# Reading turned expert outputs back over 128 rows, one scaling and scatter per step, in a fused attention and expert kernel

## The chip, the core and the metric

One core of a Trainium2 chip runs the whole program. The metric is device microseconds of one execution. Names used below: PE is the matrix engine and PEld its weight load, DVE the vector engine, ACT the scalar engine, POOL the GpSimd engine, SP the engine that issues most transfers (DMAs).

## The reference, cut to what matters

A gated linear attention feeds a gated feed-forward block, and that feeds a mixture of 8 experts. The change touches the last stage alone:

```python
def _moe2_ref(x, w_gate, w_output_gate, w1, w2):      # x: 3072 tokens x 384, 8 experts, F = 1024
    ...
    e_idx = np.argmax(logits, axis=1)                 # each token goes to one expert
    for e in range(E):
        mask = e_idx == e
        h = np.maximum(x[mask] @ w1[e], 0.0)
        ye = h @ w2[e]
        out[mask] = gate_w[mask, None] * eom[mask, e, None] * ye
```

## The kernel before, in words

Attention, feed-forward and routing fill the first 600 us and are the same in both kernels. Routing writes every token's row, its gate and its token number into a table `bucket` in DRAM, sorted by expert.

**Parts.** The experts are then worked one after the other, the fullest first. `SLOTS` gives each a shape of rows x tiles: (128,4), (114,4), (108,4), (100,4), (118,3), (112,3), (128,3), (128,3). The first is worked in two halves, so there are nine parts u = 0 to 8, and part u is slot u - 1 from u = 1 on. Each part has 8 steps j. In a step PE makes a block of h (`e_h`: 9 matmuls, L650), ACT and DVE make its two halves with relu (L1166, L1167), and two steps later `e_o` multiplies that block by w2 into three or four PSUM banks `ps_b`. All products are made three times, from a high and a low half of each operand.

**Turned parts.** Where the rows are fewer than 128 (`TURNED`: parts 2 to 6) the output is made with the model dimension on the partitions (L1187), three banks of r*n columns. The banks' unused columns up to a multiple of 32 are set to zero (L1182). `turn_out` turns the banks in 32x32 blocks on DVE (L1209) and writes them with 8 transfers into a DRAM tile `mid_o` (L1212), at step 0 of the next part. `fetch_out` at step 3 of the next part reads them back, one tile `obr` of r partitions per transfer (L1222). `fin_out` at step 6 scales all n tiles by the gates (even ones on ACT, L1231; odd ones on DVE, L1233) and scatters each by its token numbers `ix` (L1235, an indirect DMA that POOL issues). The scalings are held in source order on their engines.

**Rows of the next part.** `load_rows` reads the next part's rows from `bucket` (4 transfers of 32 partitions, L1119, and one for gates and token numbers, L1122), at step 0 of the part before it. `prep_rows` at steps 3, 5 and 6 turns them on DVE (L1134) and splits them into high and low (`x`: ACT L1147, DVE L1148), for each of three blocks kc; with the last kc it casts the token numbers to integers (L1129).

**Weights.** Eight chunks of 384 KB per expert go through six staging buffers. A chunk of w1 is split on ACT and DVE (L1075, L1076), one of w2 on ACT and POOL (L1092, L1095); the splits of one step free the buffer for a later load.

**What sets the order.** A scheduler orders each engine's instructions by a simulated timeline; what is given to `keep_in_program_order` keeps its place in the source. Each engine works its list strictly in order, so an instruction that waits holds up all behind it on that engine.

Of the kernel before, what the change touches and what calls it, by code (L numbers as in the profile page):

```python
# [8 lines left out]
F32 = mybir.dt.float32  # L9
# [46 lines left out]
def gla_glu_moe_kernel(  # L56
# [996 lines left out]
    TURNED = [p for p, (r, n) in enumerate(SLOTS) if 0 < p < E - 1 and r < P]  # L1053
    we = {}
    ring = []
    turns = [0]

    def staging(nm, shape):
# [7 lines left out]
    def load_w1(p, i):  # L1066
        n = F2 // 4
        s = slice(i * n, i * n + n)
        st = staging("st1", [P, KD, n])
        nc.sync.dma_start(st, w1.rearrange("e k n -> (e k) n")[bass.ds(places[p][1], DM), s]  # L1070
                          .rearrange("(p kc) n -> p kc n" if p else "(kc p) n -> p kc n", p=P))

        def go():
            w1h, w1l = we[p][0:2]
            for ins in (nc.scalar.activation(w1h[:, :, s], st, AF.Copy),  # L1075
                        nc.vector.tensor_tensor(out=w1l[:, :, s], in0=st, in1=f(w1h[:, :, s]), op=ALU.subtract)):  # L1076
                if p:
                    tc.keep_in_program_order(ins)
        return go

    def load_w2(p, i):
        st = staging("st2", [P, 2, DM])
        nc.sync.dma_start(st, w2.rearrange("e k n -> (e k) n")[bass.ds(places[p][2], F2), :]
                          [i * 2 * P:(i + 1) * 2 * P, :].rearrange("(kc p) n -> p kc n", p=P))

        def go():
            w2h, w2l = (w_[:, 2 * i:2 * i + 2, :] for w_ in we[p][2:4])
            src = st
            if p in TURNED:
                w2h, w2l = (w_.rearrange("p a (k m) -> p a k m", k=KD) for w_ in (w2h, w2l))  # L1090
                src = st.rearrange("p a (m k) -> p a k m", k=KD)
            ins = nc.scalar.activation(w2h, src, AF.Copy)  # L1092
            if p:
                tc.keep_in_program_order(ins)
            nc.gpsimd.tensor_tensor(out=w2l, in0=src, in1=f(w2h), op=ALU.subtract)  # L1095
        return go
# [11 lines left out]
    def load_rows(u, er):  # L1108
        p, s0, r, n = parts[u]
        rows_ = bucket[bass.ds(places[p][0], CMAX), :]  # L1110
        ix = act.tile([P, 4, 1], I32, tag="ix", name="ix", bufs=4)
        if u < 2:
            nc.sync.dma_start(er[:, 0:n, :], rows_[s0:s0 + P * n, :].rearrange("(p b) w -> p b w", b=n))
            erow[u] = (er, ix, er[:, :, DM:DM + 1], er[:, :, RW - 1:RW])
            return
        m = -(-r * n // 32)
        flat_ = flat(er)[:, 0:3 * 32 * m]
        for i in range(TW):
            nc.sync.dma_start(flat_[32 * i:32 * i + 32].rearrange("j (c w) -> j c w", c=m),  # L1119
                              rows_[0:32 * m, 96 * i:96 * i + 96].rearrange("(c j) w -> j c w", j=32))  # L1120
        eg = act.tile([P, 4, 2], F32, tag="eg", name="eg", bufs=4)
        nc.sync.dma_start(eg[0:r, 0:n, :], rows_[0:r * n, DM:RW].rearrange("(b p) w -> p b w", b=n))  # L1122
        erow[u] = (flat_, ix, eg[:, :, 0:1], eg[:, :, 1:2])

    def prep_rows(u, kc):
        _, _, r, n = parts[u]
        er, ix, _, ids = erow[u]
        if kc == (0 if u < 2 else KD - 1):
            nc.vector.tensor_copy(ix[0:r, 0:n, :], ids[0:r, 0:n, :])  # L1129
        xh, xl = x2[u]  # L1130
        if u >= 2:
            m = er.shape[1] // 96
            tc.keep_in_program_order(
                nc.vector.transpose(out=xt[:, 0:32 * m].rearrange("p (c j) -> p c j", c=m),  # L1134
                                    in_=er.rearrange("p (c d k) -> p k c d", c=m, k=KD)[:, kc]))
            psf = xt[:, 0:r * n]
        else:
            if u == 1 and kc:
                ps = psM.tile([P, n, r], F32, tag=order[kc + 1], name="ps_t")
            else:  # L1140
                ps = psE.tile([P, n, r], F32, tag="tr", name="ps_t", bufs=1)
            for i in range(n):
                ins = nc.tensor.transpose(ps[:, i, :], er[0:r, i, kc * P:kc * P + P], ident[0:r, 0:r])
                if u == 0 and i == 0:
                    tc.keep_in_program_order(ins)
            psf = ps.rearrange("p b c -> p (b c)")
        for ins in (nc.scalar.activation(xh[:, kc, :], psf, AF.Copy),  # L1147
                    nc.vector.tensor_tensor(out=xl[:, kc, :], in0=psf, in1=f(xh[:, kc, :]), op=ALU.subtract)):  # L1148
            if u == 1:
                tc.keep_in_program_order(ins)  # L1150
# [20 lines left out]
    def e_o(u, j, tiles=None):  # L1171
        p, _, r, n = parts[u]
        turned = p in TURNED
        if u not in ob2:
            ob2[u] = []
            for i in range(KD if turned else n):
                ob2[u].append(psM.tile([P, -(-r * n // 32) * 32 if turned else DM], F32,
                                       tag=order[turn[0] % 5], name="ps_b"))
                turn[0] += 1
            if turned and r * n % 32:  # L1180
                for o in ob2[u]:
                    nc.vector.memset(o[:, r * n:], 0.0)  # L1182
        hh = h2[u, j]
        if turned:
            for k_ in range(KD):
                for m, (a_, b_) in enumerate(((0, 2), (0, 3), (1, 2))):
                    nc.tensor.matmul(ob2[u][k_][:, 0:r * n], lhsT=we[p][b_][:, j, k_ * P:k_ * P + P],  # L1187
                                     rhs=hh[:, a_, :], start=(j == 0 and m == 0), stop=(j == KF2 - 1 and m == 2))
            return
        for i in range(n) if tiles is None else tiles:  # L1190
            sl = slice(i * r, i * r + r)
            for m, (a_, b_) in enumerate(((0, 2), (0, 3), (1, 2))):
                ins = nc.tensor.matmul(ob2[u][i][0:r], lhsT=hh[:, a_, sl], rhs=we[p][b_][:, j, :],  # L1193
                                       start=(j == 0 and m == 0), stop=(j == KF2 - 1 and m == 2))
                if tiles is not None:
                    tc.keep_in_program_order(ins)
# [3 lines left out]

    def turn_out(u):
        p, _, r, n = parts[u]
        nb = -(-r * n // 32)
        mid = dram.tile([4 * P, DM], F32, tag="mid_o", name="mid_o", bufs=2)
        for c0 in range(0, nb, HB):
            nc_ = min(HB, nb - c0)
            ob = act.tile([P, HB, 96], F32, tag="R", name="obt")[:, 0:nc_, :]
            for k_ in range(KD):
                nc.vector.transpose(out=ob.rearrange("p c (d k) -> p k c d", k=KD)[:, k_],  # L1209
                                    in_=ob2[u][k_][:, 32 * c0:32 * (c0 + nc_)].rearrange("p (c j) -> p c j", c=nc_))  # L1210
            for a_ in range(TW):
                nc.sync.dma_start(mid[32 * c0:32 * (c0 + nc_), 96 * a_:96 * a_ + 96].rearrange("(c j) w -> j c w", j=32),  # L1212
                                  ob[32 * a_:32 * a_ + 32])
        ob2[u, "m"] = mid

    def fetch_out(u):
        p, _, r, n = parts[u]
        ob2[u, "s"] = []
        for i in range(n):
            ob = act.tile([P, DM], F32, tag=("t", "hh", "hl")[spare[0] % 3], name="obr")  # L1220
            spare[0] += 1
            nc.sync.dma_start(ob[0:r], ob2[u, "m"][i * r:i * r + r, :])  # L1222
            ob2[u, "s"].append(ob)

    def fin_out(u):
        p, _, r, n = parts[u]
        _, ix, gates, _ = erow[u]
        for i in range(n):
            ob = ob2[u, "s"][i][0:r]
            if i % 2 == 0:  # L1230
                ins = nc.scalar.activation(ob, ob, AF.Copy, scale=gates[0:r, i, :])  # L1231
# [212 lines left out]
    def load_next(p):  # L1444
        for i in range(4):
            pw.append((load_w1, p, i))
            pw.append((load_w2, p, i))
# [27 lines left out]
    for u in range(U):  # L1475
        for j in range(KF2):
# [21 lines left out]
                load_rows(2, ers[0])  # L1498
            if u == 0 and j == 3:
                strict[0] = False  # L1500
            if u > 1 and j == 0 and u + 1 < U:
                load_rows(u + 1, ers[(u + 1) % 2])
            if u > 1 and j == 3 and parts[u][0] + 2 < E:
                addresses(parts[u][0] + 2)
                load_next(parts[u][0] + 2)
            if u and parts[u - 1][0] in TURNED and j in (3, 6):
                (fetch_out if j == 3 else fin_out)(u - 1)
            if u and u + 1 < U and j in TRJ:
                prep_rows(u + 1, TRJ.index(j))
            for _ in range(STEPS[u][j] if u < 2 else 1):  # L1510
# [10 lines left out]
        if u == 1:  # L1521
            while ready or pw:
                weight_step()
            addresses(2)
            load_next(2)
            fetch()
    op_ = overflow()
# [42 lines left out]
```

## Time and profile before

| | us |
|---|---|
| median of 3 runs | 841.31 (840.16 to 842.48) |
| profiled execution | 842.69 |
| its span | 840.9 |
| PE busy in the span | 808.4 (96%) |
| DVE, ACT, POOL busy | 549.6, 326.2, 153.2 |

PE is the bound: nearly all of the span it is busy, so a change can gain only where PE stands still or runs at a lower clock. Since the profiled execution is 1.4 us above the median, a sum is made against 842.69 and then moved to the median. Row forms: in the timeline "start us, us, engine line operation tile<-source, xcount [idle before <-what ended it]"; merged rows give the start of the first and the time from there to the end of the last.

### The profile page before, as it was taken

How to read it: one execution, taken by the hardware profiler on the slowest of the kernel's cores; microseconds unless marked ns; L12 is line 12 of the kernel's file. 1: busy time of each engine (PE TensorE's matmuls, PEld its weight loads, DVE VectorE, ACT ScalarE, POOL GpSimd, SP SyncE). 2: the span in 40 equal slices, each digit the busy share in tenths (PEclk: the TensorE clock that was granted, in tenths of full speed). 3: DMA queues.
4: the chain of work that ended last, by engine and by line, in shares of the span. 5: the costliest groups of instructions: out<-in, count | busy, mean ns of one | idle time of the engine just before them, and what ended most of it. 6: DMA issues, size and time to landing. Idle time of an engine off the chain costs nothing.

```text
span 840.9 us, 15931 instructions
## 1 busy us (share of the span) xinstructions
PE 808.4 (96%) x5967; PEld 774.8 (92%) x5967; DVE 549.6 (65%) x1202; ACT 326.2 (39%) x694; POOL 153.2 (18%) x207
## 2 busy tenths in 40 slices
PE   6999999999999999999999999999999999984996
PEld 5799999998999999999999999999988999984896
DVE  7998999498677876767766742443554765672541
ACT  1655544323333333423333323333245454452341
POOL 3000000000200110010020020013124353452351
PEclk9999999999999999999999999999999999997899
DMA  9955564863554452235454210050078667674520
GB/s 196 203 157 147 155 149 129 227 173 78 143 118 102 119 124 70 70 93 117 89 134 89 54 48 20 1 187 11 29 218 222 165 189 210 190 217 136 165 70 27
DMA packets 193751, 106.00 MB, mean 126 GB/s; under 512 B 124489, under 2 KB 188421, under 8 KB 193673
## 3 DMA queue, kind: packets, MB, share of 16 engines
q1 hardware_dynamic: 189208, 95.50, 44.8%
q0 software_dynamic: 4464, 9.48, 3.3%
q8 instruction: 47, 0.77, 0.4%
q14 instruction: 32, 0.25, 0.1%
HBM read 80.37 MB, written 24.84 MB: 125 GB/s over the span
## 4 chain that ended last, share of the span: by engine, by line
PE 76%; issue 12%; POOL 5%; DMA 3%; DVE 1%; ACT 1%; SPq 1%; POOLq 0%; DVEq 0%; ACTq 0%
PE ps_o L684 18%; PE ps_g L650 18%; PE ps_v L650 18%; PE ps_h L650 5%; PE ps_s L430 4%; PE ps_b L1187 3%; PE ps_y L468 3%; PE ps_y L464 2%; POOL w2b L1095 2%; POOL out_dram L1235 2%; POOL w2a L1095 1%; PE ps_st L489 1%; PE ps_b L1193 1%; PE pc L615 1%; DMA nat<-in_k_dram 1%
## 5 line engine op out<-in xcount | busy, mean ns | idle before, releaser
L664 ACT ACTIVATE hh<-tt 128x384 fp32r<-128x384 f32 x96 | 50.5, 526 | 145.8 <-DVE tt L661 134.8
L661 DVE TENSOR_TENSOR tt<-tt,ps_v 128x384 f32<-128x384 f32 x96 | 52.9, 551 | 82.0 <-PE ps_v L650 69.9
L642 ACT ACTIVATE tt<-ps_g 128x384 f32<-128x384 f32 x96 | 47.0, 489 | 82.2 <-PE ps_g L650 76.5
L1167 DVE SCALAR_TENSOR_TENSOR h<-ps_h,h 128x256 fp32r<-128x256 f32 (+6 forms) x72 | 37.9, 529 | 49.7 <-ACT h L1166 46.9
L670 DVE TENSOR_TENSOR hl<-tt,hh 128x384 fp32r<-128x384 f32 x96 | 54.2, 564 | 24.6 <-ACT hh L664 23.6
L650 PE MATMUL ps_g<-xh,wgh 128*128 128x384 f32 x192 | 66.5, 347 | 0.0
L650 PE MATMUL ps_v<-xh,wvh 128*128 128x384 f32 x192 | 66.4, 346 | 0.0
L684 PE MATMUL ps_o<-wol,hh 128*128 128x400 f32 x192 | 66.3, 345 | 0.0
L650 PE MATMUL ps_g<-xl,wgh 128*128 128x384 f32 x192 | 64.7, 337 | 0.9 <-DVE begin L317 0.9
L684 PE MATMUL ps_o<-woh,hh 128*128 128x400 f32 x192 | 65.3, 349 | 0.0
L650 PE MATMUL ps_h<-x,w1a 128*128 128x256 f32 (+3 forms) x288 | 53.8, 331 | 11.8 <-ACT x L1147 11.5
L650 PE MATMUL ps_v<-xh,wvl 128*128 128x384 f32 x192 | 64.8, 338 | 0.0
L650 PE MATMUL ps_g<-xh,wgl 128*128 128x384 f32 x192 | 64.6, 337 | 0.0
L650 PE MATMUL ps_v<-xl,wvh 128*128 128x384 f32 x192 | 64.5, 336 | 0.0
L684 PE MATMUL ps_o<-woh,hl 128*128 128x400 f32 x192 | 64.0, 345 | 0.0
L1166 ACT ACTIVATE h<-ps_h 128x256 fp32r<-128x256 f32 (+6 forms) x72 | 33.7, 469 | 76.7 <-PE ps_h L650 75.0
L650 PEld LDWEIGHTS ps_h<-x,w1a 128*128 128x128 f32 x288 | 48.1, 192 | 13.7 <-ACT x L1147 11.8
L650 PE MATMUL ps_h<-x,w1b 128*128 128x456 f32 (+3 forms) x288 | 57.5, 342 | 0.0
L650 PEld LDWEIGHTS ps_h<-x,w1b 128*128 128x128 f32 x288 | 50.7, 188 | 1.5
L1187 PE MATMUL ps_b<-h,w2b 128*128 128x456 f32 (+2 forms) x216 | 45.2, 352 | 2.7 <-DVE ps_b L1182 2.7
L440 DVE TENSOR_TENSOR P<-ps_s,mask 128x512 f32<-128x512 f32 x46 | 30.1, 685 | 23.6 <-PE ps_s L430 23.6
L1187 PEld LDWEIGHTS ps_b<-h,w2b 128*128 128x128 f32 x216 | 39.6, 195 | 4.3 <-issue 2.9
(312 smaller groups left out, 2011.1 us busy)
## 6 DMA issues: line engine op xcount, KB each, us to landing
st<-in_moe_w_dram SPq DMA_DIRECT2D x46, 384.0 KB
bucket<-zero SPq DMA_DIRECT2D x8, 772.0 KB
stg<-in_moe_w_gate_dram SPq DMA_DIRECT2D x12, 384.0 KB
stg<-in_moe_w_val_dram SPq DMA_DIRECT2D x12, 384.0 KB
stg<-in_moe_w_out_dram SPq DMA_DIRECT2D x12, 384.0 KB
v<-in_v_dram SPq DMA_DIRECT2D x23, 192.0 KB
more<-in_moe_w_dram SPq DMA_DIRECT2D x9, 384.0 KB
er<-in_moe_w_dram SPq DMA_DIRECT2D x9, 384.0 KB
```

The costliest lines, as they stand in the source:

```text
L430: seq(nc.tensor.matmul(ps[hh][:, p, :], lhsT=kT[r, p, :], rhs=qT[r, p, :], start=True, stop=True))
L440: pace(f'Ph{t}', nc.vector.tensor_tensor(out=Ph, in0=ps[hh], in1=mb, op=ALU.mult))
L642: nc.scalar.activation(tt, ps, AF.Silu)
L650: seq(nc.tensor.matmul(ps, lhsT=a_[:, kc, :], rhs=b_[:, kc, :], start=(n == 0), stop=(n == 3 * KD - 1)))
L661: nc.vector.tensor_tensor(out=tt, in0=tt, in1=ps, op=ALU.mult)
L664: nc.scalar.activation(hh, tt, AF.Copy)
L670: nc.vector.tensor_tensor(out=hl, in0=tt, in1=f(hh), op=ALU.subtract)
L684: seq(nc.tensor.matmul(obank[s][i], lhsT=a_[:, sl], rhs=weight(b_, j), start=(j == j0 and n == 0), stop=(j == j1 - 1 and n == 2)))
L1095: nc.gpsimd.tensor_tensor(out=w2l, in0=src, in1=f(w2h), op=ALU.subtract)
L1166: nc.scalar.activation(hh[:, 0, :], ps, AF.Relu)
L1167: nc.vector.scalar_tensor_tensor(out=hh[:, 1, :], in0=ps, scalar=0.0, in1=f(hh[:, 0, :]), op0=ALU.max, op1=ALU.subtract)
L1187: nc.tensor.matmul(ob2[u][k_][:, 0:r * n], lhsT=we[p][b_][:, j, k_ * P:k_ * P + P], rhs=hh[:, a_, :], start=(j == 0 and m == 0), stop=(j = ...
```

## The change

1. `fetch_out` reads `mid_o` back in tiles of 128 partitions; partition p of tile i takes row p*n + i (before: row i*r + p, over r partitions). So that all 128*n rows exist, the banks are 128*n columns wide, zeroed from r*n on, and all of them are turned and written. The gates and token numbers of turned parts are read with the same layout.
2. `fin_out` scales and scatters one tile per step: at steps 4 to 7 where n is 4, at 5 to 7 where n is 3.
3. `load_rows` is called at step 7 for the part after the next (before: at step 0 for the next); part 3's stays at step 0 of part 2.
4. Transfers of weights (from slot 2 on), rows, `mid_o` and `obr` keep their source order on SP.
5. The cast of the token numbers is made at step 3 of their own part.
6. The address registers of slot 2 are loaded at step 3 of part 1.

```diff
@@ load_w1, load_w2
-        nc.sync.dma_start(st, w1...)
+        ins = nc.sync.dma_start(st, w1...)
+        if p > 1:
+            pin(ins)
@@ load_rows (its four reads of the rows are pinned too)
-        nc.sync.dma_start(eg[0:r, 0:n, :], rows_[0:r * n, DM:RW].rearrange("(b p) w -> p b w", b=n))
+        pin(nc.sync.dma_start(eg[:, 0:n, :], rows_[0:P * n, DM:RW].rearrange(
+            "(p b) w -> p b w" if p in TURNED else "(b p) w -> p b w", b=n)))
@@ prep_rows
-        if kc == (0 if u < 2 else KD - 1):
+        if u < 2 and kc == 0:
             nc.vector.tensor_copy(ix[0:r, 0:n, :], ids[0:r, 0:n, :])
@@ e_o
-                ob2[u].append(psM.tile([P, -(-r * n // 32) * 32 if turned else DM], F32,
+                ob2[u].append(psM.tile([P, P * n if turned else DM], F32,
-            if turned and r * n % 32:
+            if turned:
                 for o in ob2[u]:
                     nc.vector.memset(o[:, r * n:], 0.0)
@@ turn_out (its writes of mid are pinned too)
-        nb = -(-r * n // 32)
+        nb = TW * n
@@ fetch_out
-            nc.sync.dma_start(ob[0:r], ob2[u, "m"][i * r:i * r + r, :])
+            pin(nc.sync.dma_start(ob, ob2[u, "m"][0:P * n, :].rearrange("(p b) w -> p b w", b=n)[:, i, :]))
@@ fin_out
-    def fin_out(u):
+    def fin_out(u, i):
-        for i in range(n):
+        if 0 <= i < n:
@@ the loop over parts and steps
-            if u > 1 and j == 0 and u + 1 < U:
-                load_rows(u + 1, ers[(u + 1) % 2])
-            if u > 1 and j == 3 and parts[u][0] + 2 < E:
+            if u == 2 and j == 0:
+                load_rows(3, ers[1])
+            if u > 1 and j == 7 and u + 2 < U:
+                load_rows(u + 2, ers[u % 2])
+            if u > 1 and j == 3:
+                _, _, r, n = parts[u]
+                pin(nc.vector.tensor_copy(erow[u][1][0:r, 0:n, :], erow[u][3][0:r, 0:n, :]))
+            if u and j == 3 and parts[u][0] + 2 < E:
                 addresses(parts[u][0] + 2)
-                load_next(parts[u][0] + 2)
-            if u and parts[u - 1][0] in TURNED and j in (3, 6):
-                (fetch_out if j == 3 else fin_out)(u - 1)
+                if u > 1:
+                    load_next(parts[u][0] + 2)
+            if u and parts[u - 1][0] in TURNED and j > 2:
+                if j == 3:
+                    fetch_out(u - 1)
+                fin_out(u - 1, parts[u - 1][3] - KF2 + j)
```

On ACT in the second half of part 6 stands this before (h is the relu of a step, obr the scaling of a tile of part 5, x the high half of the rows of part 7, w1a and w2a splits of weights):

```order
L1166 ACTIVATE h_9057<-ps_h 128x336
L1166 ACTIVATE h_9086<-ps_h 128x336
L1231 ACTIVATE obr<-obr,eg 118x384 x2
L1147 ACTIVATE x_7160<-xt 128x384
L1092 ACTIVATE w2a<-st_8848 128x768
L1166 ACTIVATE h_9128<-ps_h 128x336
L1092 ACTIVATE w2a<-er_6553 128x768
L1147 ACTIVATE x_7160<-xt 128x384
```

and this in the changed kernel:

```order
L1175 ACTIVATE h_9057<-ps_h 128x336
L1240 ACTIVATE obr<-obr,eg 118x384
L1156 ACTIVATE x_7160<-xt 128x384
L1100 ACTIVATE w2a<-st_8854 128x768
L1175 ACTIVATE h_9090<-ps_h 128x336
L1156 ACTIVATE x_7160<-xt 128x384
L1081 ACTIVATE w1a_6547<-st_8906 128x3x256
L1175 ACTIVATE h_9123<-ps_h 128x336
L1240 ACTIVATE obr<-obr,eg 118x384
L1100 ACTIVATE w2a<-er_6553 128x768
```

The second scaling moved from ahead of two blocks of x to behind both.

On POOL, from the end of part 4 to the start of part 6, the list before is (DMA is a scatter, four of one part in a row):

```order
L1095 TENSOR_TENSOR w2b<-st_8549,w2b 128x768
L1235 DMA out_dram<-obr,ix 3072x384 x4
L1095 TENSOR_TENSOR w2b<-st_8624,w2b 128x768
L1095 TENSOR_TENSOR w2a<-er_6553,w2a 128x768
L1095 TENSOR_TENSOR w2a<-st_8777,w2a 128x768
```

and in the changed kernel:

```order
L1244 DMA out_dram<-obr,ix 3072x384 x2
L1103 TENSOR_TENSOR w2b<-st_8555,w2b 128x768
L1244 DMA out_dram<-obr,ix 3072x384
L1103 TENSOR_TENSOR w2b<-st_8623,w2b 128x768
L1244 DMA out_dram<-obr,ix 3072x384
L1103 TENSOR_TENSOR w2a<-er_6553,w2a 128x768
L1103 TENSOR_TENSOR w2a<-st_8785,w2a 128x768
```

The split of the fourth w2b chunk moved from behind the fourth scatter to ahead of it.

On DVE at the start of part 4 the list before is (obt is the turn of part 3's banks, ps_b a bank of part 4 or 5 that is zeroed):

```order
L1209 STREAM_TRANSPOSE obt<-ps_b 128x256
L1209 STREAM_TRANSPOSE obt<-ps_b 128x192
L1182 MEMSET ps_b 128x16
L1209 STREAM_TRANSPOSE obt<-ps_b 128x256
L1209 STREAM_TRANSPOSE obt<-ps_b 128x192
L1076 TENSOR_TENSOR w1a_6548<-st_8122,w1a_6547 128x3x256
L1182 MEMSET ps_b 128x30 x2
```

and in the changed kernel:

```order
L1218 STREAM_TRANSPOSE obt<-ps_b 128x256 x6
L1082 TENSOR_TENSOR w1a_6548<-st_8122,w1a_6547 128x3x256
L1191 MEMSET ps_b 128x112
L1191 MEMSET ps_b 128x30 x2
L1176 SCALAR_TENSOR_TENSOR h_8319<-ps_h,h_8319 128x400
```

The zeroing of part 4's third bank moved behind the split of a w1 chunk, where it already stood at the start of parts 5 and 6.

## Rows read from the trace of the kernel before

**Rows 1.** Timeline of PE, 670 to 841 us.
```profile
733.43 1.73 PE L650 MATMUL ps_h<-x,w1a 128*128 128x354 f32 x9 [0.28 <-DVE h L1167]
...
750.08 1.01 PE L1187 MATMUL ps_b<-h,w2b 128*128 128x336 f32 x5 [2.66 <-DVE ps_b L1182]
...
777.08 0.69 PE L650 MATMUL ps_h<-x,w1a 128*128 128x384 f32 x1 [11.47 <-ACT x L1147]
777.57 0.76 PE L1187 MATMUL ps_b<-h,w2b 128*128 128x336 f32 x2
778.12 0.84 PE L650 MATMUL ps_h<-x,w1a 128*128 128x384 f32 x2
778.76 2.72 PE L1187 MATMUL ps_b<-h,w2b 128*128 128x336 f32 x9
781.28 2.79 PE L650 MATMUL ps_h<-x,w1a 128*128 128x384 f32 x12
784.36 1.33 PE L1193 MATMUL ps_b<-w2a,h 128*128 128x384 f32 x6 [0.29 <-ACT h L1166]
...
788.84 1.73 PE L650 MATMUL ps_h<-x,w1a 128*128 128x384 f32 x9
790.41 1.74 PE L1193 MATMUL ps_b<-w2a,h 128*128 128x384 f32 x9
...
798.53 1.32 PE L1193 MATMUL ps_b<-w2a,h 128*128 128x384 f32 x6 [1.14 <-ACT h L1166]
```

**Rows 2.** Windows: length; PE, PEld, DVE, ACT, POOL busy (count); PE clock, DMA share, GB/s.
```profile
761.70:763.50 1.80, 1.80 (x13) 1.80 (x13) 0.23 (x1) 0.00 (x0) 0.27 (x1) 1.00 0.13 50
...
777.10:779.00 1.90, 1.90 (x6) 1.90 (x7) 1.62 (x3) 1.90 (x4) 1.88 (x2) 0.50 0.17 58
...
801.00:803.00 2.00, 2.00 (x13) 2.00 (x12) 1.41 (x3) 1.06 (x2) 0.00 (x0) 1.00 0.00 0
```

**Rows 3.** Timeline around the read back of part 5, SP (issues) and ACT.
```profile
757.41 4.03 SPq L1222 DMA_DIRECT2D obr<-mid_o  x3
...
765.80 0.61 ACT L1231 ACTIVATE obr<-obr,eg 118x384 f32<-118x384 f32 x1 [4.78 <-DMA obr<-mid_o]
...
776.00 0.61 ACT L1231 ACTIVATE obr<-obr,eg 118x384 f32<-118x384 f32 x1 [9.58 <-DMA obr<-mid_o]
```

**Rows 4.** Timeline at the start of part 6: DVE, POOL and SP.
```profile
740.05 1.01 POOL L1235 DMA_INDIRECT out_dram<-obr,ix  x1 [0.16 <-ACT x L1147]
...
744.58 5.27 DVE L1076 TENSOR_TENSOR w1a<-st,w1a 128x768 fp32r<-128x768 f32 x1
...
745.20 2.07 POOL L1095 TENSOR_TENSOR w2b<-st,w2b 128x768 fp32r<-128x768 f32 x1
...
747.24 1.79 POOL L1095 TENSOR_TENSOR w2a<-er,w2a 128x768 fp32r<-128x768 f32 x1
747.30 0.38 SPq L1083 DMA_DIRECT2D st<-in_moe_w_dram  x1
747.79 5.42 SPq L1212 DMA_DIRECT2D mid_o<-obt  x8
```

**Rows 5.** Timeline in part 5: relus of steps 4 and 5, SP's issues.
```profile
728.68 0.47 ACT L1166 ACTIVATE h<-ps_h 128x354 fp32r<-128x354 f32 x1 [2.13 <-PE ps_h L650]
...
729.16 0.85 SPq L1119 DMA_DIRECT2D er<-bucket  x2
...
732.10 1.51 SPq L1222 DMA_DIRECT2D obr<-mid_o  x4
...
734.49 0.45 ACT L1166 ACTIVATE h<-ps_h 128x354 fp32r<-128x354 f32 x1
```

**Rows 6.** Timeline in part 7: read back of part 6, turn of part 8's rows.
```profile
795.63 1.34 SPq L1222 DMA_DIRECT2D obr<-mid_o  x3
796.12 0.69 DVE L1134 STREAM_TRANSPOSE xt<-er 128x384 f32<-128x384 f32 x1 [4.42 <-DMA er<-bucket]
```

**Rows 7.** Line 1209, the turns of the banks: min/median/max ns, first and last start.
```profile
L1209 DVE STREAM_TRANSPOSE obt<-ps_b x30: 250/444/558, 664.1 to 784.9; 128x256 f32<-128x256 f32 x15, 128x224 f32<-128x224 f32 x3, 128x192 f32<-128x192 f32 x3, 128x160 f32<-128x160 f32 x3
```

More of the change, by code (lines that the diff above doesn't have):

```diff
@@ L1055, in gla_glu_moe_kernel, with pin @@
     ring = []
+    def pin(ins):
+        tc.keep_in_program_order(ins)
     turns = [0]
@@ L1069, in load_w1 @@
         st = staging("st1", [P, KD, n])
-        nc.sync.dma_start(st, w1.rearrange("e k n -> (e k) n")[bass.ds(places[p][1], DM), s]
-                          .rearrange("(p kc) n -> p kc n" if p else "(kc p) n -> p kc n", p=P))
+        ins = nc.sync.dma_start(st, w1.rearrange("e k n -> (e k) n")[bass.ds(places[p][1], DM), s]
+                                .rearrange("(p kc) n -> p kc n" if p else "(kc p) n -> p kc n", p=P))
+        if p > 1:
+            pin(ins)
         def go():
@@ L1082, in load_w2 @@
         st = staging("st2", [P, 2, DM])
-        nc.sync.dma_start(st, w2.rearrange("e k n -> (e k) n")[bass.ds(places[p][2], F2), :]
-                          [i * 2 * P:(i + 1) * 2 * P, :].rearrange("(kc p) n -> p kc n", p=P))
+        ins = nc.sync.dma_start(st, w2.rearrange("e k n -> (e k) n")[bass.ds(places[p][2], F2), :]
+                                [i * 2 * P:(i + 1) * 2 * P, :].rearrange("(kc p) n -> p kc n", p=P))
+        if p > 1:
+            pin(ins)
         def go():
@@ L1118, in load_rows @@
         for i in range(TW):
-            nc.sync.dma_start(flat_[32 * i:32 * i + 32].rearrange("j (c w) -> j c w", c=m),
-                              rows_[0:32 * m, 96 * i:96 * i + 96].rearrange("(c j) w -> j c w", j=32))
+            pin(nc.sync.dma_start(flat_[32 * i:32 * i + 32].rearrange("j (c w) -> j c w", c=m),
+                                  rows_[0:32 * m, 96 * i:96 * i + 96].rearrange("(c j) w -> j c w", j=32)))
         eg = act.tile([P, 4, 2], F32, tag="eg", name="eg", bufs=4)
-        nc.sync.dma_start(eg[0:r, 0:n, :], rows_[0:r * n, DM:RW].rearrange("(b p) w -> p b w", b=n))
+        pin(nc.sync.dma_start(eg[:, 0:n, :], rows_[0:P * n, DM:RW].rearrange(
+            "(p b) w -> p b w" if p in TURNED else "(b p) w -> p b w", b=n)))
         erow[u] = (flat_, ix, eg[:, :, 0:1], eg[:, :, 1:2])
@@ L1211, in turn_out @@
             for a_ in range(TW):
-                nc.sync.dma_start(mid[32 * c0:32 * (c0 + nc_), 96 * a_:96 * a_ + 96].rearrange("(c j) w -> j c w", j=32),
-                                  ob[32 * a_:32 * a_ + 32])
+                pin(nc.sync.dma_start(mid[32 * c0:32 * (c0 + nc_), 96 * a_:96 * a_ + 96]
+                                      .rearrange("(c j) w -> j c w", j=32), ob[32 * a_:32 * a_ + 32]))
         ob2[u, "m"] = mid
@@ L1523, in gla_glu_moe_kernel @@
                 weight_step()
-            addresses(2)
             load_next(2)
```

## The prediction

> **What bounds the kernel now.** I read the busy table first: PE is busy 96% of the span, so the only thing to win is time in which PE stands still or runs at its lower clock. Then the timeline of PE over the expert parts, looking at brackets alone, since a bracket is idle time with what ended it. Five stand in the stretch that the change touches [rows 1]: 0.28 us in part 5, 2.66 at the start of part 6, 11.47 at the start of part 7, 0.29 behind that, 1.14 in the middle of part 7. Between them PE goes from matmul to matmul, so nothing else there is to be had.
>
> The large one, followed back: PE waits for ACT's x, a block of the high half of part 7's rows [rows 1]. ACT was free for it long before, but its list is in order and two scalings of part 5's rows stand right ahead: one started at 765.80 after 4.78 us of waiting for its read from mid_o, the other at 776.00 after 9.58 us [rows 3]. SP had issued these three reads from 757.41 on. So the end of the chain is a transfer that took up to 18.6 us. The DMA window shows why: while little else moved, 0.13 of the DMA engines were busy at 50 GB/s [rows 2], and 0.13 is two of sixteen. Part 5's tiles have 118 rows. Two engines at 50 GB/s need 3.6 us for one tile (118 x 384 x 4 bytes, 0.18 MB) and 10.9 for three, and the weight chunks need those two engines as well.
>
> **The change part by part.**
>
> *Read back over 128 partitions.* It takes the whole 11.47 us if the reads land in time. The nearest row for a read on more engines is part 6's, three tiles of 112 rows: issued from 795.63, and from 801.0 to 803.0 no DMA moved anything [rows 2, 6], so three tiles and what was queued around them landed within 5.4 us. The first scaling waits for that, and the last one, which held up x, now stands behind both blocks of x on ACT, as the order in part 6 shows. Added work: more columns to turn. Second halves of 224, 192, 160, 128 and 96 columns become 256, 256, 256, 128 and 128, three banks each, 672 columns in all; at 0.444 us for a turn of mostly 256 [rows 7] that is 1.2 us over five parts, on DVE, which is busy 65% of the span; writes and reads grow by a tenth or less. I set it to nothing, because PE does not wait for the turned tiles but for a free bank; without that cover it would cost the 1.2 us.
>
> The Trainium skill, in "DMA: Bandwidth & Descriptors", section "Why a DMA increments its semaphore by 16 and not by 1", says that a transfer runs on the largest number of engines up to 16 that divides the outer sizes of both its sides. By it 118 rows give 2, 112 give 16, 114, 108 and 100 give 6, 12 and 10, and 128 give 16. The 0.13 agrees; no run here shows the other counts. By it the reads of parts 2 to 4 gain little and part 6's nothing, which leaves the sum as it is.
>
> *Lower clock.* Behind the long idle time PE ran at 0.50, its 1.2 GHz level [rows 2]. From 777.08 to 784.07 (784.36 less 0.29) it did 15 matmuls of 384 columns (1 + 2 + 12) and 11 of 336 (2 + 9) [rows 1]. At full clock nine of 384 take 790.41 - 788.84 = 1.57 us [rows 1], so 0.174 each and, by columns, 0.153 for 336: 2.61 + 1.68 = 4.29. It took 6.99, so 2.70 us were lost, and they go with the stall. With the 0.29 behind it, an echo of the same stall, this place gives 11.47 + 2.70 + 0.29 = **14.46**.
>
> *Rows read one part earlier, ahead of mid_o on SP.* In part 7 DVE waits for part 8's rows until 796.12 [rows 6], ACT's x waits for DVE, the relu stands behind x, and PE loses 1.14 [rows 1]. The rows will have landed a part before. **1.14** goes. The same chain causes the 0.28 of part 5: **0.28**. What is late next on that path is x itself, whose turn has no other source to wait for.
>
> *Scatters one per step.* The 2.66 us wait is for the zeroing of a bank, behind a split of w1 on DVE that took 5.27 us. While it ran, POOL made two splits of w2, from 745.20 to 747.27 and from 747.24 to 749.03; DVE ended 0.8 us later [rows 4]. DVE's two-input instruction stands still as long as POOL's runs. The first of these splits stood behind four scatters; in the new order it stands ahead of the last. The four held POOL from 740.05 to 745.20 [rows 4], 1.3 us each, so it moves forward by one to three of them, clear of DVE's split or nearly; the second may still touch it. I count **2.66** as gone, with 0 as the other end. SP gains too: its load at 747.30, ahead of the mid_o writes, follows the end of POOL's first split at 747.27 [rows 4], so mid_o starts earlier.
>
> The Trainium skill, in "GPSIMD Engine Reference", section "8. Key points", says that GpSimd shares its SBUF interfaces with the vector engine and contends with instructions that have two SBUF inputs. The 5.27 us agrees. The rule speaks against part of this change: a rival below.
>
> *First scaling at step 4, one step after the read.* This is the wait that is added. Worst is part 5, with four tiles and the shortest steps. There ACT is through the relu of step 4 at 729.15 and comes to the scaling; the reads went out at 732.10 before [rows 5], and up to 2.9 us sooner (729.16) with the reads of rows gone from ahead of them. With 5.4 us for landing, ACT waits until 734.6 to 737.5 at worst, and much less if the first tile lands in half that. Behind the scaling on ACT stand a w1 split and the relu of step 5, which came at 734.49 before [rows 5]. PE goes on meanwhile, since h is used two steps later and ps_h has two banks. So the loss is 0 to some 2 us in part 5, less in parts 3 and 4 with their longer steps: 0 to 4 together. I take 1.2, nearer the low end for the two banks.
>
> *Casts, pins, registers.* The cast waits for token numbers that were read a part before, and no longer stands ahead of x; its cover is a full part. If that is gone, it stands before DVE's turn of rows, at the price of rows landing late, 1.14. The pins leave the weight loads in nearly the old order: one w2 load now follows the reads of rows. On SP behind each stand the mid_o writes, 5.42 us of issuing [rows 4], and then obr. Nothing.
>
> **Sum.** 14.46 + 2.66 + 1.14 + 0.28 = 18.54, less 1.2: 17.3. The profiled execution took 842.69, so 825.4; the median of the runs is 1.4 lower, so **824.0**.
>
> **The rivals.**
>
> *ACT waits for the round trip.* The first scalings of parts 3, 4 and 5 come before their reads have landed, and PE stands for it, say 2.5 us each. For it: mid_o alone takes 5.42 us to issue, and the read needs all of it. Against: the two banks, and that mid_o starts earlier. 7.5 instead of 1.2: 830.3.
>
> *DVE and POOL collide elsewhere.* The zeroing of part 4's third bank now stands behind a split of w1, as those of parts 5 and 6 did. If a split of w2 falls on that, PE waits as in [rows 4], 2.66, there and still in part 6: 824.0 + 2 x 2.66 = 829.3. "GPSIMD Engine Reference" of the Trainium skill, named above, would have it so wherever both run.
>
> *The change doesn't do what it says.* The read is late for another cause than the two engines, the weight chunks ahead of it, and half of the 14.46 stays: 831.2. Against it stands 50 GB/s at 0.13 while nothing was queued but these.
>
> *Slower.* POOL's list ties the loop together: a scatter that waits for its scaling holds up the split of w2 behind it, that split frees the buffer for which SP's load waits, and that load stands ahead of the mid_o writes, on which the next scaling depends. If the round trip exceeds the four steps from turning to the last scatter, each of parts 3 to 7 ends later by the excess. It decides against the change from 18.5 / 5 = 3.7 us a part; with 4.3 it gives 841.3 + 3 = 844.3. For it: SP did wait for POOL at 747.30 [rows 4]. Against: issuing mid_o (5.42) and reading (5.4 at most) make 11 us, and eight steps of 18 matmuls at 0.174 make 25.
>
> **How the numbers follow.** Forecast 0.68, round trip 0.13, collision 0.10, change without effect 0.05, slower 0.04. The range: at the low end all 18.5 are gone, 822.8, and runs lie 1.2 below their median, 821.6; at the high end the rivals up to 831. Within 0.3% (2.5 us, about what a measurement can tell from no change) lies little of this: faster 0.93, same 0.03, slower 0.04.
>
> **What the new profile would show.** Right: no bracket over 3 us on PE in parts 3 to 8, clock 1.00 there, obr scalings of part 5 with brackets under 3 us, no bracket for er on DVE. The read is settled by the DMA share behind its issue: far above 0.13. The 2.66 is settled by the first split of w1 in part 6: 1 us or 3 and more. The round trip shows as ACT's brackets "DMA obr" and PE's "ACT h" in parts 3 to 5. Wrong would be a new bracket of 5 us or more on PE, or part 7 starting late again.

## The result, and the profile after

The changed kernel took 822.57 us (median, 821.73 to 824.23), the kernel before beside it 841.89: a ratio of 0.9776, with a 95% interval of 0.9752 to 0.9799. Two later comparisons gave 0.9808 and 0.9802 (below), so the change is worth 16 to 19 us (18.9, 16.1 and 16.6 by the three ratios). Forecast were 824.0 us, that is 17.3 less than before.

The profiled execution took 821.73 us, its span is 819.9. The busy table of the changed kernel, first part of the page:

```profile
PE 804.4 (98%) x5967; PEld 772.2 (94%) x5967; DVE 539.0 (66%) x1202; ACT 326.3 (40%) x694; POOL 153.8 (19%) x207
```

PE is busy 4.0 us less than before and the span is 21.0 shorter. The timeline of PE, with the first matmuls of part 2 and the last 18 of `ps_h` as marks, and the only bracket that is left between them:

```profile
630.01 1.40 PE L650 MATMUL ps_h<-x,w1b 128*128 128x456 f32 x6
...
635.56 1.52 PE L1196 MATMUL ps_b<-h,w2b 128*128 128x456 f32 x6 [0.29 <-ACT h L1175]
...
802.88 3.29 PE L650 MATMUL ps_h<-x,w1b 128*128 128x384 f32 x18
```

All five brackets of [rows 1] are gone. The same two marks stand in the kernel before at

```profile
631.88 1.40 PE L650 MATMUL ps_h<-x,w1b 128*128 128x456 f32 x6
...
823.85 3.29 PE L650 MATMUL ps_h<-x,w1b 128*128 128x384 f32 x18
```

so the stretch went from 191.97 to 172.87 us: 19.10 less. The five brackets and the lower clock make 18.54, 0.29 is new, and 0.85 more went in small pieces that I did not follow. Of the 21.0 in span, 1.9 lies ahead of the first mark: two executions of nearly the same code, of which the one before had a granted clock of 0.97 in its first 50 us, the one after 1.00.

The read back of part 5, which answers to [rows 3], in the timeline of SP and ACT:

```profile
750.89 1.29 SPq L1231 DMA_DIRECT2D obr<-mid_o  x3
...
754.57 0.62 ACT L1240 ACTIVATE obr<-obr,eg 118x384 f32<-118x384 f32 x1 [1.01 <-DMA obr<-mid_o]
755.09 0.51 ACT L1156 ACTIVATE x<-xt 128x384 fp32r<-128x384 f32 x1
...
761.40 0.60 ACT L1240 ACTIVATE obr<-obr,eg 118x384 f32<-118x384 f32 x1
```

The first tile is there 3.7 us after its issue, the last is not waited for. The windows behind that issue, to be held against 0.13 and 50 GB/s in [rows 2], with PE's clock, the DMA share and GB/s at the end:

```profile
751.00:752.30 1.30, 1.30 (x11) 1.30 (x10) 1.07 (x2) 0.68 (x1) 1.30 (x1) 1.00 0.92 289
752.30:754.60 2.30, 2.30 (x17) 2.30 (x16) 2.07 (x3) 0.49 (x2) 0.23 (x1) 1.00 1.02 352
```

And the start of part 6 on POOL and DVE, which answers to [rows 4]:

```profile
739.08 2.09 POOL L1103 TENSOR_TENSOR w2b<-st,w2b 128x768 fp32r<-128x768 f32 x1 [0.90 <-ACT w2b L1100]
...
742.40 0.92 DVE L1082 TENSOR_TENSOR w1a<-st,w1a 128x768 fp32r<-128x768 f32 x1
...
743.32 0.10 DVE L1191 MEMSET ps_b<- 128x48 f32 x1
...
743.75 1.86 POOL L1103 TENSOR_TENSOR w2a<-er,w2a 128x768 fp32r<-128x768 f32 x1 [1.41 <-ACT w2a L1100]
```

POOL's two splits stand on either side of DVE's, which takes 0.92 us and not 5.27.

So the sum came out. Whether each term came from the part of the change to which the prediction gave it is another question, and there the experiments say something else.

### The profile page after: what moved, and what is told of

Same layout as the page of the kernel before. It is cut to its first block, busy times and chain, and to the rows that moved or that the text cites. A ratio compares the mean times of both kernels' runs of the same rounds, so it can differ in the third digit from the quotient of the medians.

```text
span 819.9 us, 15933 instructions
## 1 busy us (share of the span) xinstructions
PE 804.4 (98%) x5967; PEld 772.2 (94%) x5967; DVE 539.0 (66%) x1202; ACT 326.3 (40%) x694; POOL 153.8 (19%) x207
## 4 chain that ended last, share of the span: by engine, by line
PE 94%; issue 2%; DVE 1%; DMA 1%; POOL 1%; ACT 0%; POOLq 0%; DVEq 0%; ACTq 0%; SPq 0%
PE ps_o L684 19%; PE ps_g L650 19%; PE ps_v L650 18%; PE ps_h L650 12%; PE ps_b L1196 8%; PE ps_b L1202 4%; PE ps_s L430 3%; PE ps_y L468 3%; PE ps_y L464 2%; PE ps_st L489 1%; PE pc L615 1%; PE ps_n L283 1%; PE junk L860 1%; PE ps_k L450 1%; DMA er<-bucket 0%
## 5 line engine op out<-in xcount | busy, mean ns | idle before, releaser
L475 POOL TENSOR_SCALAR ss<-ss 128x1 f32<-128x1 f32 x24 | 9.8, 410 | 186.4 <-ACT xn L474 183.1
```

## The experiments

| kernel | median us | before beside it | ratio, 95% interval |
|---|---|---|---|
| e1 before, 120 rows in slot 4 | 830.59 | 839.77 | 0.9872 (0.9840 to 0.9903) |
| e2 before, 122 rows | 842.13 | 839.77 | 1.0020 (1.0005 to 1.0034) |
| e3 before, read over 128 rows | 827.16 | 839.77 | 0.9843 (0.9815 to 0.9871) |
| e4 changed, read over r rows | 831.62 | 839.77 | 0.9901 (0.9871 to 0.9931) |
| e5 changed | 823.50 | 840.47 | 0.9808 (0.9773 to 0.9842) |
| e6 changed, scalings at step 6 | 821.36 | 840.47 | 0.9780 (0.9753 to 0.9807) |
| e7 changed, rows read at step 0 | 829.57 | 840.47 | 0.9877 (0.9849 to 0.9905) |
| e8 changed, scalings a step sooner | 826.52 | 840.47 | 0.9849 (0.9820 to 0.9878) |
| e9 before, two splits on DVE | 837.65 | 840.35 | 0.9963 (0.9948 to 0.9978) |
| e10 before, 128 rows and rows early | 824.09 | 840.35 | 0.9818 (0.9794 to 0.9843) |
| e11 as e6 | 822.50 | 840.35 | 0.9792 (0.9774 to 0.9811) |
| e12 changed | 823.74 | 840.35 | 0.9802 (0.9781 to 0.9823) |

**Is it the two DMA engines?** One size, nothing moved:

```diff
-    SLOTS = [(P, 4), (114, 4), (108, 4), (100, 4), (118, 3), (112, 3), (P, 3), (P, 3)]
+    SLOTS = [(P, 4), (114, 4), (108, 4), (100, 4), (120, 3), (112, 3), (P, 3), (P, 3)]
```

> The kernel before with one size changed: the fifth slot has 120 rows x 3 tiles instead of 118 x 3. All engines keep their order. 144 matmuls of part 5 get 6 columns more, at 0.45 ns a column (1.57 us for nine of 384) 0.4 us. Theory (a read of 118 rows runs on two DMA engines): by the Trainium skill's rule, 'DMA: Bandwidth & Descriptors', 'Why a DMA increments its semaphore by 16 and not by 1', 120 rows give 15 engines; worked out from the trace alone, the 11.47 + 2.70 + 0.29 = 14.46 us at the start of part 7 go, so 841.9 - 14.46 + 0.4 = 827.8, the three reads land within 5 us, and the DMA share behind their issue is far above 0.13. Rival (the read is late because weight chunks stand ahead of it, or because of its place in the order): order and chunks are the same, so 842.3.

and the same with `(122, 3)`:

> The same with 122 rows x 3 tiles, 12 columns more in 144 matmuls: 0.8 us. Theory (it is the divisor of the row count): 122 is twice a prime, as 118 is, so two engines again: share 0.13, the wait for x at the start of part 7 stays at 11.5 to 12.5 (a read 3% longer), time 842.7 to 844. Rival (any row count but 118 would do, or a larger tile is read faster): the stall goes, 828.2.

The read back of part 5 with 120 rows (e1), timeline of SP and ACT, and the windows behind its issue:

```profile
758.58 1.33 SPq L1222 DMA_DIRECT2D obr<-mid_o  x3
...
764.05 0.62 ACT L1231 ACTIVATE obr<-obr,eg 120x384 f32<-120x384 f32 x1 [0.26 <-DMA obr<-mid_o]
...
765.73 0.62 ACT L1231 ACTIVATE obr<-obr,eg 120x384 f32<-120x384 f32 x1 [1.07 <-DMA obr<-mid_o]
...
760.20:762.00 1.80, 1.80 (x14) 1.80 (x13) 0.94 (x3) 1.44 (x3) 0.10 (x1) 1.00 0.96 330
```

and with 122 (e2), with PE's bracket at the start of part 7:

```profile
756.28 4.37 SPq L1222 DMA_DIRECT2D obr<-mid_o  x3
...
764.51 0.62 ACT L1231 ACTIVATE obr<-obr,eg 122x384 f32<-122x384 f32 x1 [2.81 <-DMA obr<-mid_o]
...
775.52 0.61 ACT L1231 ACTIVATE obr<-obr,eg 122x384 f32<-122x384 f32 x1 [10.40 <-DMA obr<-mid_o]
...
760.70:762.50 1.80, 1.80 (x13) 1.80 (x13) 1.03 (x2) 0.45 (x1) 0.96 (x1) 1.00 0.14 55
...
776.60 0.69 PE L650 MATMUL ps_h<-x,w1a 128*128 128x384 f32 x1 [10.32 <-ACT x L1147]
```

Two rows more and the three tiles land within 7.2 us, at a share of 0.96; four rows more and it is 0.14 again, 19.2 us to the last scaling and the stall is back. It is 10.32 us, below the 11.5 to 12.5 expected; by the ratio e2 is 1.7 us slower than before, within what was expected. The order on every engine is the same in both, so it is the row count, and not the chunks or the place: the rival that the change doesn't do what it says is out. The rule of the Trainium skill that the prediction named ("DMA: Bandwidth & Descriptors", "Why a DMA increments its semaphore by 16 and not by 1") gives 15 engines for 120 rows and 2 for 122. The 0.14 agrees with two. The 0.96, and the 0.92 to 1.02 with 128 rows, rule out a few engines but can't tell 15 from 16, since weight chunks run beside the read.

e1 gained 10.8 us by its ratio where 14.1 were expected. The rest is seen in its trace, timeline of DVE, POOL and PE in part 7:

```profile
768.61 1.86 POOL L1095 TENSOR_TENSOR w2a<-st,w2a 128x768 fp32r<-128x768 f32 x1
...
769.01 3.69 DVE L1148 TENSOR_TENSOR x<-xt,x 128x384 fp32r<-128x384 f32 x1 [0.54 <-issue]
...
770.42 1.86 POOL L1095 TENSOR_TENSOR w2a<-er,w2a 128x768 fp32r<-128x768 f32 x1
...
772.76 0.96 PE L650 MATMUL ps_h<-x,w1a 128*128 128x384 f32 x4 [0.78 <-DVE x L1148]
```

The low half of x, 0.56 us elsewhere, meets POOL's next two splits and takes 3.69. This is the rival "collide elsewhere", with 0.78 on PE and two brackets of 0.3 behind it. The wait for `ps_b` in part 6 stays (2.50), and here the clock fell behind it, which it had not done in the profile before; that is told below, and it costs some 1.5 us. By an estimate from e1's rows, 14.46 less all these, less 0.5 us more of waiting in part 5 and 0.4 for the wider rows, with 0.7 us less of waiting elsewhere, is about 11.

**The read alone, and everything but the read.** e3 is the kernel before with only the first point of the change (layout of `obr` and `eg`, banks of 128*n columns). e4 is the changed kernel with the read undone, and with it the layout of the gates and token numbers (not printed); its banks stay 128*n columns wide:

```diff
-            pin(nc.sync.dma_start(ob, ob2[u, "m"][0:P * n, :].rearrange("(p b) w -> p b w", b=n)[:, i, :]))
+            pin(nc.sync.dma_start(ob[0:r], ob2[u, "m"][i * r:i * r + r, :]))
```

> The kernel before with the read-back layout of the changed kernel alone: 128 partitions per tile, banks of 128*n columns, the rest as before (both scalings of a part at step 6, rows read at step 0, cast with the last block of x, no pins). With it the scheduler also moves the second scaling of part 5 behind one block of x. Theory (14.46 us hang on the read, the other 4.1 on scatters and rows): 841.9 - 14.46 = 827.4, PE still waits 2 to 3 us for ps_b at the start of part 6 and about 1 us for ACT in the middle of part 7. Rival (the gain needs the scalings spread over the steps): the stall at part 7 is only halved, 834 or more.

> The changed kernel with that part undone: tiles read back with r rows each (114, 108, 100, 118, 112), all else as changed; every engine keeps the changed order. Theory (two engines for 118 rows, and the wait falls on whatever stands behind a scaling): the three reads of part 5 again take some 4 us for the first to 11 to 18 us for the last; the first scaling now stands ahead of one block of x only, and the third ahead of a w2 split and a relu. PE loses part of the 11.5: 826, between 823 and 833. Rival (one scaling per step is what removed the stall, and the read's speed does not matter): 822.6 within 1.

e3 came out at 0.9843, 13.2 us where 14.5 were expected, but not with the brackets expected. Timeline of e3, start of part 6 and end of part 6:

```profile
742.45 2.11 POOL L1095 TENSOR_TENSOR w2b<-st,w2b 128x768 fp32r<-128x768 f32 x1
743.12 2.27 DVE L1076 TENSOR_TENSOR w1a<-st,w1a 128x768 fp32r<-128x768 f32 x1
...
744.66 2.46 POOL L1095 TENSOR_TENSOR w2a<-er,w2a 128x768 fp32r<-128x768 f32 x1
...
762.38 3.56 DVE L1076 TENSOR_TENSOR w1a<-st,w1a 128x768 fp32r<-128x768 f32 x1 [0.17 <-ACT w1a L1075]
...
763.25 1.86 POOL L1095 TENSOR_TENSOR w2a<-st,w2a 128x768 fp32r<-128x768 f32 x1
...
766.41 0.73 PE L1187 MATMUL ps_b<-h,w2b 128*128 128x336 f32 x3 [2.34 <-DVE h L1167]
```

PE does not wait for `ps_b`, although four scatters stand in a row as before: POOL comes to its split 0.7 us ahead of DVE instead of 0.6 behind [rows 4]. Another collision has come up twenty microseconds later and costs PE 2.34 us. All five brackets of [rows 1] are gone, the 1.14 and the 0.28 too, although e3 reads its rows at step 0: DVE waits 3.35 us for them in part 7, PE does not. So the expected time came out by luck. More went than the 14.46, and new brackets of 2.34 and 0.34 took much of that back; between the two marks above e3 needs 176.80 us, 15.17 less than before.

e4 lost half of the gain. Timeline of SP and ACT around part 5's read, and PE's two brackets:

```profile
752.36 4.00 SPq L1231 DMA_DIRECT2D obr<-mid_o  x3
756.56 4.00 SPq L1074 DMA_DIRECT2D st<-in_moe_w_dram  x1
760.72 0.61 ACT L1240 ACTIVATE obr<-obr,eg 118x384 f32<-118x384 f32 x1 [6.76 <-DMA obr<-mid_o]
...
762.87 1.84 PE L1196 MATMUL ps_b<-h,w2b 128*128 128x336 f32 x6 [3.47 <-ACT h L1175]
...
771.07 0.61 ACT L1240 ACTIVATE obr<-obr,eg 118x384 f32<-118x384 f32 x1 [3.44 <-DMA obr<-mid_o]
...
772.84 1.23 PE L1202 MATMUL ps_b<-w2a,h 128*128 128x384 f32 x4 [1.80 <-ACT h L1175]
```

Every engine's order is that of the changed kernel, yet the last scaling comes 18.7 us after the issue and the wait falls on the relus behind both scalings: 5.27 us of brackets, and behind each of them a stretch at 0.50 of the clock (764 to 766, 774 to 776), which makes most of the rest of 9.4 in span. So spreading the scalings does not replace the fast read; it splits the stall in two.

**Spread, early rows, pins.** e6 puts all scalings and scatters back to step 6, e7 reads the rows at step 0 again, e8 makes each scaling one step sooner, e5 is the changed kernel beside them:

```diff
 e6 (and e11)
-                fin_out(u - 1, parts[u - 1][3] - KF2 + j)
+                for i in range(parts[u - 1][3] if j == 6 else 0):
+                    fin_out(u - 1, i)
 e7
-            if u == 2 and j == 0:
-                load_rows(3, ers[1])
-            if u > 1 and j == 7 and u + 2 < U:
-                load_rows(u + 2, ers[u % 2])
+            if u > 1 and j == 0 and u + 1 < U:
+                load_rows(u + 1, ers[(u + 1) % 2])
 e8
-                fin_out(u - 1, parts[u - 1][3] - KF2 + j)
+                fin_out(u - 1, parts[u - 1][3] - KF2 + j + 1)
```

> The changed kernel once more, beside its variants on one chip: 0.978 of before, 821 to 823.

> The changed kernel with the scalings and scatters of a part all at step 6 again; reads over 128 rows, early rows and pins stay. On POOL four scatters stand in a row, and behind them at the start of part 6 the two w2 splits. Theory of the prediction (the spread of the scatters removes the 2.66): the w1 split of DVE there takes 3 to 5 us beside POOL's, PE waits 2 to 3 us for ps_b, and where the clock falls behind it 1.5 more: 2.5 to 4.5 above the changed kernel. Rival (with the read over 128 rows alone that wait was gone too, four scatters in a row or not: when POOL gets there depends on when the reads land): within 1 us of the changed kernel.

> The changed kernel with the rows of the next part read at step 0 of the part before, as in the kernel before; all else as changed. Theory (1.14 + 0.28 come from rows that land late): DVE waits for er by 3 to 5 us again in part 7, PE gets brackets of about 1.1 and 0.3 for ACT's or DVE's h, so 1 to 2 us above the changed kernel. Rival (the rows are not what PE waited for, or the reads land in time once SP's list is shorter): within 0.5.

> The changed kernel with every scaling and scatter one step sooner (from step 3 where n is 4, in the step of the read; from step 4 where n is 3). It exposes the round trip through mid_o. Theory (ACT waits, PE does not, since h is used two steps later): ACT's waits for obr grow from 6.0 us to 12 or more, PE loses less than 1.5 us in all. Rival of the prediction (PE stands for the round trip): 2.5 us for each of parts 3 to 5, 7.5 above the changed kernel, with PE brackets that end with ACT h.

*e5* came out at 0.9808, where 0.978 was expected, and at 823.50 us, half a microsecond above the range.

*e6* is as fast as the changed kernel. The 2.66 does not come back; at the start of part 6 its POOL and DVE read

```profile
736.07 1.00 POOL L1244 DMA_INDIRECT out_dram<-obr,ix  x1 [0.18 <-issue]
...
741.43 2.08 POOL L1103 TENSOR_TENSOR w2b<-st,w2b 128x768 fp32r<-128x768 f32 x1
...
742.41 1.94 DVE L1082 TENSOR_TENSOR w1a<-st,w1a 128x768 fp32r<-128x768 f32 x1
...
743.73 2.34 POOL L1103 TENSOR_TENSOR w2a<-er,w2a 128x768 fp32r<-128x768 f32 x1 [0.22 <-ACT w2a L1100]
```

The first of the four scatters starts 6.3 us ahead of DVE's split; before it was 4.5 [rows 4]. In e3 it is 5.6, in e10 below 6.7; in e1 and e2, where PE waits for `ps_b` too, 4.7 and 4.8. So a longer lead goes with no wait in these six kernels, all with four scatters in a row there, and it comes from what lands sooner, not from spreading. The rows suggest how. With the longer lead POOL's first split ends at about the time when ACT has made the high half for the second (`ACT w2a` above). That leaves a gap of 0.10 us (e3), 0.22 (e6) or 0.41 (e10) between POOL's two splits, and DVE's goes through there. Before, the second followed the first without a gap (747.27 and 747.24, [rows 4]), and DVE waited for both.

*e7* loses 6 us (0.9877 against 0.9808) where 1 to 2 were expected. Timeline of DVE and PE in part 7, and of POOL and DVE at the end of part 5:

```profile
785.28 0.68 DVE L1143 STREAM_TRANSPOSE xt<-er 128x384 f32<-128x384 f32 x1 [7.07 <-DMA er<-bucket]
...
786.45 1.97 PE L650 MATMUL ps_h<-x,w1a 128*128 128x384 f32 x7 [1.96 <-DVE h L1176]
...
738.38 4.37 POOL L1103 TENSOR_TENSOR w2b<-st,w2b 128x768 fp32r<-128x768 f32 x2
...
740.76 2.81 DVE L1082 TENSOR_TENSOR w1b<-more,w1b 128x768 fp32r<-128x768 f32 x1
...
744.06 1.25 PE L1196 MATMUL ps_b<-h,w2a 128*128 128x354 f32 x3 [1.63 <-DVE h L1176]
```

In part 7 it is the wait of the kernel before: the rows stand behind the writes of `mid_o` on SP and land 5 us after their issue. But DVE, probably since the stall at the start of the part is gone and it is less behind, waits 7.07 us for them and not 4.42 [rows 6], and PE 1.96 and not 1.14. The missing stall alone does not explain it, since it is missing in e3 too; SP's writes of `mid_o` ahead of the rows take 7.64 us to issue in e7, 6.04 before and 4.93 in e3. The rest is lost in part 5, where two of POOL's splits run in one stretch of 4.37 us against DVE and PE waits 1.96 (for x, at 740.89) and 1.63, with the clock at 0.50 from 744 to 749. The scheduler also put the blocks of x later on ACT in e7, and what of this second place is the late rows and what the new order was not taken apart.

*e8* exposes the round trip. What ACT and DVE wait for the read (view by tile `obr`), in the changed kernel and in e8, in us and times:

```profile
  DMA obr<-mid_o: 6.0, 4
```

```profile
  DMA obr<-mid_o: 17.3, 7
```

PE pays for it with brackets of 0.37, 0.36, 0.44, 1.29 and 0.24, all ended by ACT; in time 3.4 us (0.9849 against 0.9808; the two intervals overlap a little), between the 1.5 and the 7.5 expected.

**Does DVE stand still beside POOL?** e9 takes POOL's two splits out of the kernel before:

```diff
-            nc.gpsimd.tensor_tensor(out=w2l, in0=src, in1=f(w2h), op=ALU.subtract)
+            (nc.vector if (p, i) in ((5, 3), (6, 0)) else nc.gpsimd).tensor_tensor(out=w2l, in0=src, in1=f(w2h), op=ALU.subtract)
```

> The kernel before with two of POOL's splits of w2 given to DVE: the last chunk of slot 5 and the first of slot 6, the two that ran on POOL beside DVE's slow w1 split at the start of part 6. Theory (DVE's two-input instruction stands still beside POOL's): the w1 split there takes 0.9 to 1.0 us instead of 5.27, the two splits cost DVE 1 us each, PE's wait of 2.66 for ps_b falls to 0 to 1, so 839 to 841.5 if the rest stays (the scheduler also moves two blocks of x of part 7 ahead on ACT, which may take some of the 11.47). Rival (the w1 split is slow by itself, by its data or by the transfers that run then): 3 us or more again, and PE waits longer than before, since DVE has 2 us more to do.

The same instruction on DVE, timeline of e9, and PE's bracket in part 7:

```profile
745.28 0.93 DVE L1076 TENSOR_TENSOR w1a<-st,w1a 128x768 fp32r<-128x768 f32 x1
...
775.71 0.69 PE L650 MATMUL ps_h<-x,w1a 128*128 128x384 f32 x1 [12.13 <-ACT x L1147]
```

0.93 instead of 5.27, no wait for `ps_b`, 3.1 us gained by the ratio (0.4 to 2.9 expected), and the stall of part 7 stays. Held against how long POOL's splits ran before DVE's got through, worked out from the rows: before 3.83 us [rows 4] and 4.3 longer; e1 at 769.01 3.27 and 3.1; e3 at 743.12 1.44 and 1.3; e6 1.10 and 1.0; e9 none and none. In e3 and e6 that is POOL's first split alone. The second overlaps DVE's too, and there POOL's is the longer one: 2.46 and 2.34 us, where it took 1.79 before. So the two don't run side by side: whichever waits gets longer by about the time for which the other is at work.

**How little of the change does it.** e10 is the kernel before with the read over 128 rows and the early rows alone; e11 and e12 repeat e6 and the changed kernel with more rounds:

> The kernel before with two parts of the change: tiles of 128 partitions, and rows read at step 7 for the part after the next. No pins, scalings and scatters together at step 6, casts where they were. Theory (these two make the gain, spread and pins none of it): 821 to 823, no PE bracket above 0.5 in parts 3 to 8. Rival (the pins, which hold mid_o and obr in their place among the weight chunks, carry part of it): 824 to 828 with a bracket of 1 us or more.

> The changed kernel with scalings and scatters together at step 6, once more and with more rounds: as good as the changed kernel or 1 to 2 us better, 820.5 to 822.

> The changed kernel beside it: 821 to 824, with more spread than the one before, as far as the first comparison goes.

e10, at 0.9818, can't be told from the changed kernel (0.9802, 0.9808), though its median of 824.09 is above the 821 to 823 expected. Its one PE bracket in parts 3 to 8 is 0.75, where 0.5 at most was expected; it stands behind a wait of DVE of 4.49 us for `eg` at the cast of the token numbers, the cast that the full change moves. Pins, spread and the moved cast are worth less than these runs resolve. So is what the early rows add to the read alone: 15.3 us (e10) against 13.2 (e3), with intervals that overlap. e6 and e11 stand 1 to 2 us below the changed kernel beside them, but the intervals overlap: as good with simpler code, not shown to be better.

## Why the prediction was right, and where its steps were not

The largest term was right and the sum came out, but in part by luck: the other 4.08 us (2.66, 1.14, 0.28) were given to the spread and to the early rows, and in e3 they went with the read alone.

**The 14.46 (11.47, 2.70, 0.29).** Right in cause and, as far as the runs separate it, in size. 120 against 122 rows settles the cause. For the size there are the brackets, which are gone, and e1: 10.8 us gained, against some 11 by its own rows. e3's 13.2 us do not test it, since other brackets went there too and new ones came. The first tile landed 3.7 us after its issue, within the 5.4 taken from part 6.

**The 2.66.** Right that it goes and that DVE stood still beside POOL, which e9 shows directly. Wrong step: "in the new order it stands ahead of the last". In the changed kernel POOL's first split does end before DVE's starts, but its place among the scatters is not needed, since e6, e3 and e10 have four in a row and don't wait either. What counts is when POOL's list gets there, and an earlier read is enough for that. The order printed for the changed kernel showed a moved row, and I took the move for the cause.

**The 1.14 and the 0.28.** Both went, but the two brackets are not the worth of the early rows, in either direction. e3 has neither, with rows still read at step 0. In the changed kernel undoing the early rows costs 6 us, not 1.4: in part 7 DVE waits 7.07 us for them, and in part 5 late rows go along with POOL's splits on top of DVE's, which no bracket of before showed. Why late rows cost so little in e3 and so much in e7, where scalings are spread and transfers pinned, no run takes apart. So I would now price a wait that stands beside a larger one with a range to both sides.

**The charge of 1.2 for the scaling at step 4.** About zero. ACT did wait for the read, 6.0 us in four waits, the longest 3.16, and no bracket on PE follows from it: 172.87 us between the marks with one bracket of 0.29, in part 2. That the two banks cover it, as argued, no run shows by itself. e8 gives the limit: with one step less, the waits grow to 17.3 and cost 3.4 us. With the charge at zero the forecast would have been 822.8, 18.5 us less than before; by the ratios it was 18.9, 16.1 and 16.6 less. So the trace shows that the charge was not needed, and the times are too far apart to show it.

**The rivals.** The round trip shows only with the scalings a step sooner (e8). "Collide elsewhere" is the one that came nearest: in e1, e3 and e7 a collision of DVE and POOL comes up at another place, at 0.8 to 2.3 us of PE each. In the changed kernel one is there too and costs nothing: timeline of DVE and POOL in part 6,

```profile
757.12 2.15 DVE L1242 TENSOR_SCALAR obr<-obr,eg 118x384 f32<-118x384 f32 x1
757.18 1.86 POOL L1103 TENSOR_TENSOR w2a<-st,w2a 128x768 fp32r<-128x768 f32 x1
```

A scaling that takes 0.41 us elsewhere takes 2.15, and x behind it is still in time. In two other profiled executions (e5, e12) it reached PE with 0.15 us. "Slower" found no support: no bracket on PE in parts 3 to 7.

## What to carry to other kernels

When a transfer is slow while little else moves, look at the DMA share behind its issue before looking at its place in the queue, and try the row count: here two rows more were worth 11 us with nothing else changed. A term that rests on two engines getting in each other's way is a term on timing; expect it to turn up elsewhere when the timing moves, and test it by taking one of the two away. Undo each part of a change from the changed kernel, not only add it to the old one: the early rows were worth 1.4 us by the old brackets and 6 by the undoing, while the read alone had already taken those brackets away.

## What the runs showed of the hardware that was not expected

**A read on two engines holds the queue that issues it.** In e4 the three reads of 118 rows take SP 4.00 us to issue and the weight chunk behind them another 4.00; with 128 rows it is 1.29 and 0.55. So all that SP issues behind such a read starts late too. Scatters of such row counts take longer too: POOL is 1.63 to 1.69 us busy with each of those of 118 and 122 rows, 1.00 to 1.01 with those of 120 (e1), and 0.94 to 1.35 with those of the other turned parts before. Whether it is for the same reason no row tells.

**The clock behind a wait of 2.5 us.** In the kernel before PE went on at 1.00, its 2.4 GHz level, behind the 2.66. In e1 and e2 it fell to 0.50, 1.2 GHz, at the same place behind waits of 2.50 and 2.35, in e3 at another place behind 2.34. Windows of e1 behind it:

```profile
753.00:754.00 1.00, 1.00 (x5) 1.00 (x5) 0.00 (x0) 0.00 (x0) 0.00 (x0) 0.50 0.29 69
```

Nine matmuls of 336 columns took 2.72 us there and 1.54 in the kernel before. What decides it these runs don't tell. So such a wait can cost 1.2 us more on these nine alone, or not.

**DVE is held up by POOL also in a scaling.** "GPSIMD Engine Reference", section "8. Key points", of the Trainium skill speaks of DVE instructions with two SBUF inputs or in a mode that uses two ports. The splits agree; the scaling at 757.12 has one tile as input and a column of gates, and was longer by 1.74 us with POOL's split beside it for 1.86. Whether it runs in such a mode no row here tells.
